# A dense SiLU feed-forward layer on one core: the first loads cut in two over both queues, the first group of matmuls taken by halves of the rows

## The chip, the cores and the metric

One NeuronCore of a Trainium2 chip runs the whole kernel in a single launch. The metric is the device time in microseconds, lower is better. The shorthand for the engines is that of the profile: PE is TensorE's matmul, PEld its weight load, DVE is VectorE, ACT is ScalarE, POOL is GpSimd, and SP is SyncE, which issues DMAs and computes nothing. A "q" behind an engine's name (SPq, ACTq) marks a DMA that this engine issued.

## The reference

All arrays are bf16. x has 2048 rows of 640, w1 is 640 x 1728, and w2 is 1728 x 640.

```python
def reference(x, w1, w2):
    h = jnp.einsum("bsd,df->bsf", x, w1)
    h = _silu(h)
    out = jnp.einsum("bsf,fd->bsd", h, w2)
    return out
```

## The kernel before, in words

**Shapes.** The contraction of the first product, 640, is five tiles of 128 (`dt` 0 to 4). The 1728 columns of w1 are thirteen full tiles of 128 (`ft` 0 to 12) and one half tile. The 2048 rows of x are four chunks of 512 (`sc` 0 to 3). The first product is made transposed: a matmul takes a 128x128 block of w1 as the stationary operand and 128x512 of the transposed x as the moving one, and five of them (one for each `dt`) add up in one of the eight PSUM banks. ACT takes the sigmoid out of the bank (L197) and DVE multiplies it with the bank (L200), which gives the hidden layer, transposed, in SBUF. The second product (L319) reads that as it lies.

**Order.** Nothing is scheduled by a program: `Plan.add` records the operations, each engine runs its own in the order in which they were added, and a wait is put before an operation whose dependence comes from another engine or from a DMA. Each engine's queue is in order, so what stands behind a waiting instruction waits too.

**The opening**, which is what the change touches. The first chunk of x (512 rows, four row tiles `j`) is loaded in plain form into `x0_sb` and transposed on PE with an identity (`transpose_x0`, L174), 128x128 at a time into a PSUM bank, from which one engine copies it to `xT_sb`: DVE for even `dt` (L178), ACT for odd ones (L180). `dt` 0 is done in two halves of two row tiles each, both copied by DVE; the other four are copied whole, 128x512. The other three chunks come transposed by DMA later (L235).

The DMAs of the opening are issued in this order. SP: x tile 0, row tiles 0 and 1 (64 KB); w1 tile 0 of the contraction, its first six column tiles (192 KB, `w1_0`); the same of w1 tiles 1 and 2; then, after a wait for both halves of x tile 0, w1 tiles 3 and 4; then the remaining columns of w1 in two pieces. ACT: x tile 0, row tiles 2 and 3 (64 KB); x tile 1 (128 KB); x tile 2 (128 KB); x tiles 3 and 4 together (256 KB); then the load of its sigmoid table and a small activation (L155).

PE's list at the opening is: six matmuls on constants whose results nobody reads (L164, five of 512 columns and one of 256); the four transposes of x tile 0; two more matmuls on constants (512 and 256 columns); and then the first column group, `column_group(0, ...)`: six column tiles of w1 in six banks, with the contraction tile as the outer loop, so that each of the thirty matmuls (L258) needs only the contraction tiles that have come so far. In each contraction tile, after the second of the six matmuls, the four transposes of the next x tile are put in (`between`). The first matmul of a contraction tile waits for the copied x tile and for its w1 tile. Behind the group come the column tiles 6 to 12 of the same rows (`unit`, L213), and then the other chunks.

The matmuls on constants use the last bank, the transposes of x tile 0 use banks 4 and 5, and those of the later x tiles use bank 6 or 7 in turn.

Of the kernel before, what the change touches and what calls it, by code (L numbers as in the profile page):

```python
# [20 lines left out]
class Plan:  # L21
# [53 lines left out]
def bass_standalone__dense_activation_silu__prompt_kernel(  # L75
# [6 lines left out]
    bf16 = mybir.dt.bfloat16  # L82
# [6 lines left out]
    P = 128  # L89
    H = P // 2  # L90
    SCH = 512
    DT = D // P
# [5 lines left out]
    JB = SCH // P  # L98
# [4 lines left out]
    with ExitStack() as es:  # L103
        def sb(name, shape, dtype):
            return es.enter_context(nc.sbuf_tensor(name, shape, dtype))

        xT_sb = sb("xT_sb", [P, DT, S], bf16)
        w1_sb = sb("w1_sb", [P, DT, F], bf16)
# [16 lines left out]
        add = plan.add  # L125
        bank_free = [[] for _ in range(NBANK)]
        turn = [0]

        def take_bank():
            b = turn[0] % NBANK  # L130
            turn[0] += 1
            return b


        FA = 6
        w1_cuts = [FA, 10, FT]
        id_a = add("pool", lambda e: e.memset(ident[:, :], 0.0))
        id_b = add("pool", lambda e: e.affine_select(
            out=ident[:, :], in_=ident[:, :], compare_op=ALU.not_equal, fill=1.0,
            base=0, pattern=[[-1, P]], channel_multiplier=1), [id_a])  # L140
        warm = add("dve", lambda e: e.memset(warm_sb[:, :], 0.0))

        def load_x0(eng, name, j0, j1, d0, d1):
            return add(eng, lambda e: e.dma_start(
                out=x0_sb[:, j0:j1, d0 * P:d1 * P], in_=x0_v[:, j0:j1, d0 * P:d1 * P]), group=name)

        def load_w1(eng, name, d0, d1, f0, f1, deps=()):
            return add(eng, lambda e: e.dma_start(
                out=w1_sb[:, d0:d1, f0:f1], in_=w1_v[:, d0:d1, f0:f1]), deps, group=name)

        x0_a = [load_x0("sp", "x0_a", 0, JB // 2, 0, 1), load_x0("act", "x0_b", JB // 2, JB, 0, 1)]
        w1_lo = [load_w1("sp", "w1_0", 0, 1, 0, FA * P)]
        x0_c = [load_x0("act", "x0_c", 0, JB, 1, 2), load_x0("act", "x0_d", 0, JB, 2, 3), load_x0("act", "x0_e", 0, JB, 3, DT)]
        w1_lo += [load_w1("sp", f"w1_{dt}", dt, dt + 1, 0, FA * P) for dt in (1, 2)]
        add("act", lambda e: e.activation(out=warm_sb[:, :], in_=warm_sb[:, :], func=ACT.Sigmoid), [warm])  # L155
        w1_lo += [load_w1("sp", f"w1_{dt}", dt, dt + 1, 0, FA * P, x0_a) for dt in (3, 4)]
        w1_dma = [load_w1("sp", f"w1_{name}", 0, DT, w1_cuts[g] * P, min(w1_cuts[g + 1] * P, F))
                  for g, name in enumerate("ab")]
# [3 lines left out]
        def warm_up(columns):  # L162
            for n in columns:
                add("pe", lambda e, n=n: e.matmul(  # L164
                    ps[:, NBANK - 1, 0:n], lhsT=ones[:, 0:P], rhs=ones[:, 0:n], start=True, stop=True))

        warm_up([SCH] * 5 + [2 * P])

        def transpose_x0(dt, j0, j1, b):

            dst = ps[:, b, :].bitcast(bf16)[:, j0 * P:j1 * P]
            out = xT_sb[:, dt, j0 * P:j1 * P]
            for j in range(j0, j1):
                t = add("pe", lambda e, j=j: e.transpose(  # L174
                    dst[:, (j - j0) * P:(j - j0 + 1) * P], x0_sb[:, j, dt * P:(dt + 1) * P], ident[:, :]),
                    [x0_a[j // (JB // 2)], id_b] if dt == 0 else [x0_c[min(dt, 3) - 1]] + bank_free[b])
            if dt % 2 == 0:
                c = add("dve", lambda e: e.tensor_copy(out=out, in_=dst), [t])  # L178
            else:
                c = add("act", lambda e: e.copy(out=out, in_=dst), [t])  # L180
            bank_free[b] = [c]
            return c

        def x_deps(sc, c0, n):
            return x0T if sc == 0 else x1_of if sc == 1 else [x_dma[sc]]

        def w1_deps(ft):
            return [w1_dma[max(g for g in range(len(w1_dma)) if w1_cuts[g] <= ft)]] if ft >= FA else w1_lo

        chunk_done, tail_done = {}, {}  # L190
        sig_free = [None] * NSIG
# [2 lines left out]
        def silu(b, parts, n, pe):  # L194
            s = sig_turn[0] % NSIG
            sig_turn[0] += 1
            a = add("act", lambda e: e.activation(  # L197
                out=sig_sb[:, s, 0:n], in_=ps[:, b, 0:n], func=ACT.Sigmoid), [pe, sig_free[s]])
            for rows, ft, cols in parts:
                v = add("dve", lambda e, rows=rows, ft=ft, cols=cols: e.tensor_tensor(  # L200
                    out=hT_sb[rows, ft, cols], in0=ps[rows, b, 0:n], in1=sig_sb[rows, s, 0:n],
                    op=ALU.mult), [a])
                chunk_done[cols.start // SCH] = v
                if ft == FR:
                    tail_done[cols.start // SCH] = v
            bank_free[b] = [v]
            sig_free[s] = v

        def unit(sc, ft, c0, n):
            b = take_bank()  # L210
            cols = slice(sc * SCH + c0, sc * SCH + c0 + n)
            for dt in range(DT):
                pe = add("pe", lambda e, dt=dt: e.matmul(  # L213
                    ps[:, b, 0:n], lhsT=w1_sb[:, dt, ft * P:(ft + 1) * P], rhs=xT_sb[:, dt, cols],
                    start=(dt == 0), stop=(dt == DT - 1)),
                    x_deps(sc, c0, n) + w1_deps(ft) + bank_free[b] if dt == 0 else ())
            silu(b, [(slice(0, P), ft, cols)], n, pe)

        def tail_unit(sc):
            b = take_bank()  # L220
            for dt in range(DT):
                for hh in range(2):
                    pe = add("pe", lambda e, dt=dt, hh=hh: e.matmul(  # L223
                        ps[hh * H:(hh + 1) * H, b, :], lhsT=w1_sb[:, dt, FR * P:F],
                        rhs=xT_sb[:, dt, (sc + hh) * SCH:(sc + hh + 1) * SCH],
                        start=(dt == 0), stop=(dt == DT - 1), skip_group_check=True),
                        x_deps(sc, 0, SCH) + x_deps(sc + 1, 0, SCH) + w1_deps(FR) + bank_free[b]
                        if dt == 0 else ())
            silu(b, [(slice(hh * H, (hh + 1) * H), FR, slice((sc + hh) * SCH, (sc + hh + 1) * SCH))
                     for hh in range(2)], SCH, pe)  # L230

        x_dma, x1_of, w2_dma = {}, [], []
        for sc in range(1, NSC):
            for dt in range(DT):
                x_dma[sc] = add("sp", lambda e, sc=sc, dt=dt: e.dma_start_transpose(  # L235
                    out=xT_sb[:, dt, sc * SCH:(sc + 1) * SCH],
                    in_=xf[sc * SCH:(sc + 1) * SCH, dt * P:(dt + 1) * P]),
# [3 lines left out]
            if sc == 2:  # L241
                half = FR // 2
                for a, z in ((0, half), (half, FR)):
                    w2_dma.append(add("sp", lambda e, a=a, z=z: e.dma_start(
                        out=w2_sb[:, a:z, :], in_=w2_v[:, a:z, :]), group="w2"))
                for hh in range(2):
                    w2_dma.append(add("sp", lambda e, hh=hh: e.dma_start(
                        out=w2_sb[hh * H:(hh + 1) * H, FR, :], in_=w2[FR * P:F, :]), group="w2"))

        def column_group(sc, x_dep, w1_dep, between=None):  # L250

            banks = [take_bank() for _ in range(FA)]
            for dt in range(DT):
                for ft in range(FA):
                    deps = bank_free[banks[ft]] if dt == 0 else []
                    if ft == 0:
                        deps = deps + [x_dep[dt], w1_dep[dt]]
                    pe = add("pe", lambda e, dt=dt, ft=ft: e.matmul(  # L258
                        ps[:, banks[ft], :], lhsT=w1_sb[:, dt, ft * P:(ft + 1) * P],
                        rhs=xT_sb[:, dt, sc * SCH:(sc + 1) * SCH],  # L260
                        start=(dt == 0), stop=(dt == DT - 1)), deps)
                    if dt == DT - 1:
                        silu(banks[ft], [(slice(0, P), ft, slice(sc * SCH, (sc + 1) * SCH))], SCH, pe)
                    if between and ft == 1:
                        between(dt + 1)

        def transpose_next(dt):
            if dt < DT:
                x0T.append(transpose_x0(dt, 0, JB, FA + dt % 2))

        half = [transpose_x0(0, k * JB // 2, (k + 1) * JB // 2, FA - 2 + k) for k in range(2)]
        x0T = [half[1]]
        warm_up([SCH, 2 * P])
        column_group(0, x0T, w1_lo, transpose_next)
        for ft in range(FA, FR):
            unit(0, ft, 0, SCH)

        for sc in range(1, NSC):
            if sc == 1:
                column_group(sc, x1_of, w1_lo)  # L280
            for ft in range(FA if sc == 1 else 0, FR):
                unit(sc, ft, 0, SCH)
        reg_done = dict(chunk_done)
# [111 lines left out]
```

## Time and profile before

| What | Value |
|---|---|
| three runs | 126.38, 126.88 and 129.13 us; median 126.88 |
| the profiled execution's own time | 126.5 us |
| its span, first to last instruction | 125.2 us |
| around the span | 1.3 us |
| PE busy | 122.1 us, 98% of the span |
| PEld busy | 57.4 us, 46% |
| DVE and ACT busy | 45.6 us (36%) and 39.4 us (32%) |
| DMA | 10.41 MB in 19625 packets |

The page has one part for each question: the busy time of each engine, the same in 40 slices, the DMA queues, the chain of work that ended last, the costliest groups of instructions, and the DMA issues with the median time from issue to landing. The trace also answers by stretches of time (the timeline, in which neighbouring instructions of one line are merged: start, length, engine, line, names, count, and in brackets the idle time before and what ended it). A landing below is the start of the issue plus the time to landing. The end of a matmul is modelled and reaches into the next one, so what the array takes for one matmul is read from the distance between two starts.

### The profile page before, as it was taken

The page shows a single profiled execution, that of the slowest core. Times are in us where ns is not written, and L with a number is a line of the kernel's source. Part 1 is how long each engine was busy: PE and PEld are TensorE (multiplying, and loading weights), DVE is VectorE, ACT ScalarE, POOL GpSimd, SP SyncE. Part 2 cuts the span into 40 slices and gives each one's busy share as a digit, 9 for nine tenths or more (in the row PEclk, how much of TensorE's full clock was granted, in tenths as well). Part 3 has the DMA queues.
Part 4 walks back from the last instruction along what each step waited for, and adds up shares of the span by engine and source line. Part 5 has one row for each costly group of instructions (what it writes and reads, how often), then busy time and mean ns, then how long its engine had stood idle before and what let it go on. Part 6 is the DMA issues. An engine that isn't in the chain of part 4 may idle for free.

```text
span 125.2 us, 2101 instructions
## 1 busy us (share of the span) xinstructions
PE 122.1 (98%) x902; PEld 57.4 (46%) x902; DVE 45.6 (36%) x72; ACT 39.4 (32%) x69; POOL 0.7 (1%) x6
## 2 busy tenths in 40 slices
PE   7999999999999999999999999999999999999992
PEld 2544444444444444444444444444444444445481
DVE  0112986069766666666673020202020120202022
ACT  0523953087555555555540010101010110101021
POOL 2000000000000000000000000000000000000000
PEclk9999999999999999999999999999999999999999
DMA  3995355589910000000000001114120200112424
GB/s 77 314 385 181 86 113 72 112 237 390 276 43 0 5 0 0 3 0 0 0 0 5 0 0 31 26 22 168 52 105 5 105 0 21 26 21 73 157 98 117
DMA packets 19625, 10.41 MB, mean 83 GB/s; under 512 B 13344, under 2 KB 19616, under 8 KB 19616
## 3 DMA queue, kind: packets, MB, share of 16 engines
q1 hardware_dynamic: 17472, 9.56, 26.6%
q10 hardware_dynamic: 2144, 0.72, 2.2%
q8 instruction: 7, 0.11, 0.4%
q14 instruction: 2, 0.02, 0.1%
HBM read 5.16 MB, written 2.62 MB: 62 GB/s over the span
## 4 chain that ended last, share of the span: by engine, by line
PE 98%; DVE 0%; issue 0%
PE ps L319 47%; PE ps L213 34%; PE ps L258 11%; PE ps L164 3%; PE ps L223 2%; PE ps L174 1%; DVE o_sb L330 0%
## 5 line engine op out<-in xcount | busy, mean ns | idle before, releaser
L319 PE MATMUL ps<-w_sb,hT_sb 64*128 64x512 bf16 (+2 forms) x486 | 47.3, 352 | 0.0
L200 DVE TENSOR_TENSOR hT_sb<-ps,sig_sb 128x512 bf16<-128x512 f32 (+1 forms) x56 | 37.0, 688 | 19.0 <-ACT sig_sb L197 18.9
L213 PE MATMUL ps<-xT_sb,w_sb 128*128 128x512 bf16 x200 | 43.5, 379 | 0.0
L197 ACT ACTIVATE sig_sb<-ps 128x512 bf16<-128x512 f32 x54 | 30.7, 606 | 24.9 <-PE ps L213 16.4
L319 PEld LDWEIGHTS ps<-w_sb,hT_sb 64*128 64x128 bf16 x486 | 23.3, 94 | 23.7
L213 PEld LDWEIGHTS ps<-xT_sb,w_sb 128*128 128x128 bf16 x200 | 19.6, 98 | 23.6
L330 DVE CAST o_sb<-ps 128x512 bf16<-128x512 f32 (+2 forms) x9 | 5.7, 632 | 37.6 <-PE ps L319 37.6
L332 ACT CAST o_sb<-ps 128x512 bf16<-128x512 f32 (+2 forms) x9 | 4.8, 538 | 38.6 <-PE ps L319 38.6
L258 PE MATMUL ps<-xT_sb,w_sb 128*128 128x512 bf16 x60 | 14.4, 387 | 0.0
L319 PE MATMUL ps<-hT_sb,w_sb 64*128 64x512 bf16 x108 | 12.3, 376 | 0.0
L258 PEld LDWEIGHTS ps<-xT_sb,w_sb 128*128 128x128 bf16 x60 | 5.6, 99 | 6.7 <-DVE xT_sb L178 0.7
L319 PEld LDWEIGHTS ps<-hT_sb,w_sb 64*128 64x128 bf16 x108 | 5.2, 94 | 6.6 <-issue 0.4
L330 DVE CAST oT_sb<-ps 128x512 bf16<-128x512 f32 x2 | 1.4, 692 | 11.7 <-PE ps L319 11.7
L332 ACT CAST oT_sb<-ps 128x512 bf16<-128x512 f32 x2 | 1.2, 586 | 13.6 <-PE ps L319 13.6
L178 DVE COPY xT_sb<-ps 128x256 bf16<-128x256 bf16 (+1 forms) x4 | 1.4, 358 | 8.6 <-PE ps L174 8.6
L164 PE MATMUL ps<-const-bfloat16-1.0 128*128 128x512 bf16 (+1 forms) x8 | 3.3, 572 | 0.8 <-PEq L380 0.8
L174 PEld LDWEIGHTS ps<-ident,x_sb 128*128 128x128 bf16 x20 | 1.9, 115 | 1.7 <-DMA x_sb<-in_x_dram 0.7
L174 PE MATMUL ps<-ident,x_sb 128*128 128x128 bf16 x20 | 2.4, 256 | 0.0
L180 ACT COPY xT_sb<-ps 128x512 bf16<-128x512 bf16 x2 | 1.2, 585 | 3.9 <-PE ps L174 3.9
L223 PE MATMUL ps<-xT_sb,w_sb 128*64 128x512 bf16 x20 | 2.3, 381 | 0.0
L155 ACT ACT_TABLE_LOAD x1 | 1.3, 1283 | 2.9 <-issue 2.9
L164 PEld LDWEIGHTS ps<-const-bfloat16-1.0 128*128 128x128 bf16 x8 | 1.0, 137 | 1.9 <-issue 1.9
(9 smaller groups left out, 2.3 us busy)
## 6 DMA issues: line engine op xcount, KB each, us to landing
out_dram<-o_sb SPq DMA_DIRECT2D x14, 160.0 KB, 1.9
w_sb<-in_w_dram SPq DMA_DIRECT2D x1, 1120.0 KB, 7.6
w_sb<-in_w_dram SPq DMA_DIRECT2D x5, 192.0 KB, 4.8
w_sb<-in_w_dram SPq DMA_DIRECT2D x1, 960.0 KB, 5.3
w_sb<-in_w_dram SPq DMA_DIRECT2D x1, 640.0 KB, 6.3
w_sb<-in_w_dram SPq DMA_DIRECT2D x1, 560.0 KB, 7.3
x_sb<-in_x_dram ACTq DMA_DIRECT2D x2, 128.0 KB, 3.8
x_sb<-in_x_dram ACTq DMA_DIRECT2D x1, 256.0 KB, 5.8
```

Source lines behind the costliest of these rows:

```text
L155: add("act", lambda e: e.activation(out=warm_sb[:, :], in_=warm_sb[:, :], func=ACT.Sigmoid), [warm])
L164: add("pe", lambda e, n=n: e.matmul(ps[:, NBANK - 1, 0:n], lhsT=ones[:, 0:P], rhs=ones[:, 0:n], start=True, stop=True))
L174: t = add("pe", lambda e, j=j: e.transpose(dst[:, (j - j0) * P:(j - j0 + 1) * P], x0_sb[:, j, dt * P:(dt + 1) * P], ident[:, :]), [x0_a[j ...
L178: c = add("dve", lambda e: e.tensor_copy(out=out, in_=dst), [t])
L197: a = add("act", lambda e: e.activation(out=sig_sb[:, s, 0:n], in_=ps[:, b, 0:n], func=ACT.Sigmoid), [pe, sig_free[s]])
L200: v = add("dve", lambda e, rows=rows, ft=ft, cols=cols: e.tensor_tensor(out=hT_sb[rows, ft, cols], in0=ps[rows, b, 0:n], in1=sig_sb[rows, ...
L213: pe = add("pe", lambda e, dt=dt: e.matmul(ps[:, b, 0:n], lhsT=w1_sb[:, dt, ft * P:(ft + 1) * P], rhs=xT_sb[:, dt, cols], start=(dt == 0), ...
L223: pe = add("pe", lambda e, dt=dt, hh=hh: e.matmul(ps[hh * H:(hh + 1) * H, b, :], lhsT=w1_sb[:, dt, FR * P:F], rhs=xT_sb[:, dt, (sc + hh) * ...
L258: pe = add("pe", lambda e, dt=dt, ft=ft: e.matmul(ps[:, banks[ft], :], lhsT=w1_sb[:, dt, ft * P:(ft + 1) * P], rhs=xT_sb[:, dt, sc * SCH:( ...
L319: pe = add("pe", lambda e, b=b, n=n, lhsT=lhsT, rhs=rhs, ft=ft: e.matmul(ps[:, b, 0:n], lhsT=lhsT, rhs=rhs, start=(swap == 0 and ft == 0), ...
L330: ev = add("dve", lambda e, b=b, n=n, dst=dst: e.tensor_copy(out=dst, in_=ps[:, b, 0:n]), [pe])
L332: ev = add("act", lambda e, b=b, n=n, dst=dst: e.copy(out=dst, in_=ps[:, b, 0:n]), [pe])
```

## The change

Three things are done in the opening; from the second column group on the code does what it did.

1. The loads. `w1_0`, 192 KB, becomes two DMAs of 96 KB: column tiles 0 to 2 on SP, 3 to 5 on ACT. x tile 1, 128 KB, becomes two of 64 KB: row tiles 0 and 1 on SP, 2 and 3 on ACT. SP so has x tile 0 (first half), w1_0 (first half), x tile 1 (first half), w1 tiles 1 and 2, and the rest as before. ACT has x tile 0, w1_0 and x tile 1 (second halves each), x tile 2, x tiles 3 and 4, and then its table.
2. The first contraction tile of the first column group is done by halves of the rows: six matmuls of 256 columns for the first 256 rows and six for the other 256, in place of six of 512. Each waits only for its half of x and its half of w1_0. The transposes of x tile 1 now stand behind the fourth of the twelve. The second of the two matmuls on constants ahead of the group, the one of 256 columns, is left out.
3. Each x tile is transposed into two banks (4 and 5 for tile 0, 6 and 7 for all others), two row tiles in each, and copied as two pieces of 128x256: both by DVE for tile 0, one by DVE and one by ACT for the others.

```diff
-        w1_lo = [load_w1("sp", "w1_0", 0, 1, 0, FA * P)]
-        x0_c = [load_x0("act", "x0_c", 0, JB, 1, 2), load_x0("act", "x0_d", 0, JB, 2, 3), load_x0("act", "x0_e", 0, JB, 3, DT)]
-        w1_lo += [load_w1("sp", f"w1_{dt}", dt, dt + 1, 0, FA * P) for dt in (1, 2)]
+        w1_0 = [load_w1("sp", "w1_0a", 0, 1, 0, FA // 2 * P), load_w1("act", "w1_0b", 0, 1, FA // 2 * P, FA * P)]
+        x0_b = [load_x0("sp", "x0_c", 0, JB // 2, 1, 2), load_x0("act", "x0_d", JB // 2, JB, 1, 2)]
+        x0_c = [load_x0("act", "x0_e", 0, JB, 2, 3), load_x0("act", "x0_f", 0, JB, 3, DT)]
+        w1_lo = [load_w1("sp", f"w1_{dt}", dt, dt + 1, 0, FA * P) for dt in (1, 2)]
...
-        def transpose_x0(dt, j0, j1, b):
-
-            dst = ps[:, b, :].bitcast(bf16)[:, j0 * P:j1 * P]
-            out = xT_sb[:, dt, j0 * P:j1 * P]
-            for j in range(j0, j1):
-                t = add("pe", lambda e, j=j: e.transpose(
-                    dst[:, (j - j0) * P:(j - j0 + 1) * P], x0_sb[:, j, dt * P:(dt + 1) * P], ident[:, :]),
-                    [x0_a[j // (JB // 2)], id_b] if dt == 0 else [x0_c[min(dt, 3) - 1]] + bank_free[b])
-            if dt % 2 == 0:
-                c = add("dve", lambda e: e.tensor_copy(out=out, in_=dst), [t])
-            else:
-                c = add("act", lambda e: e.copy(out=out, in_=dst), [t])
-            bank_free[b] = [c]
-            return c
+        def transpose_x0(dt, b0):
+
+            copies = []
+            for h in range(2):
+                dst = ps[:, b0 + h, :].bitcast(bf16)[:, 0:SCH // 2]
+                out = xT_sb[:, dt, h * (SCH // 2):(h + 1) * (SCH // 2)]
+                load = (x0_a[h], x0_b[h], x0_c[0], x0_c[1], x0_c[1])[dt]
+                for k in range(2):
+                    t = add("pe", lambda e, k=k, h=h, dst=dst: e.transpose(
+                        dst[:, k * P:(k + 1) * P], x0_sb[:, 2 * h + k, dt * P:(dt + 1) * P], ident[:, :]),
+                        [load, id_b] + bank_free[b0 + h])
+                if h == 0 or dt == 0:
+                    c = add("dve", lambda e, dst=dst, out=out: e.tensor_copy(out=out, in_=dst), [t])
+                else:
+                    c = add("act", lambda e, dst=dst, out=out: e.copy(out=out, in_=dst), [t])
+                bank_free[b0 + h] = [c]
+                copies.append(c)
+            return copies
...
             for dt in range(DT):
-                for ft in range(FA):
-                    deps = bank_free[banks[ft]] if dt == 0 else []
-                    if ft == 0:
-                        deps = deps + [x_dep[dt], w1_dep[dt]]
...
+                by_half = between is not None and dt == 0
+                for h in range(2 if by_half else 1):
+                    c0, c1 = (h * (SCH // 2), (h + 1) * (SCH // 2)) if by_half else (0, SCH)
+                    for ft in range(FA):
+                        deps = [x_dep[dt][h], w1_dep[dt][ft >= FA // 2]] if by_half else []
+                        if not by_half and ft == 0:
+                            deps = x_dep[dt] + w1_dep[dt]
+                        if dt == 0 and h == 0:
+                            deps = deps + bank_free[banks[ft]]
+                        pe = add("pe", lambda e, dt=dt, ft=ft, h=h, c0=c0, c1=c1: e.matmul(
+                            ps[:, banks[ft], c0:c1], lhsT=w1_sb[:, dt, ft * P:(ft + 1) * P],
+                            rhs=xT_sb[:, dt, sc * SCH + c0:sc * SCH + c1],
+                            start=(dt == 0 and h == 0), stop=(dt == DT - 1), skip_group_check=True), deps)
+                        if dt == DT - 1:
+                            silu(banks[ft], [(slice(0, P), ft, slice(sc * SCH, (sc + 1) * SCH))], SCH, pe)
+                        if between and h == 0 and ft == (3 if by_half else 1):
+                            between(dt + 1)
...
-        half = [transpose_x0(0, k * JB // 2, (k + 1) * JB // 2, FA - 2 + k) for k in range(2)]
-        x0T = [half[1]]
-        warm_up([SCH, 2 * P])
-        column_group(0, x0T, w1_lo, transpose_next)
+        x0T = [transpose_x0(0, FA - 2)]
+        warm_up([SCH])
+        w1_of = [w1_0] + [[d] for d in w1_lo]
+        column_group(0, x0T, w1_of, transpose_next)
```

More of the change, by code (lines that the diff above doesn't have):

```diff
@@ L167, in bass_standalone__dense_activation_silu__prompt_kernel @@
         warm_up([SCH] * 5 + [2 * P])
-        def transpose_x0(dt, j0, j1, b):
-            dst = ps[:, b, :].bitcast(bf16)[:, j0 * P:j1 * P]
-            out = xT_sb[:, dt, j0 * P:j1 * P]
-            for j in range(j0, j1):
-                t = add("pe", lambda e, j=j: e.transpose(
-                    dst[:, (j - j0) * P:(j - j0 + 1) * P], x0_sb[:, j, dt * P:(dt + 1) * P], ident[:, :]),
-                    [x0_a[j // (JB // 2)], id_b] if dt == 0 else [x0_c[min(dt, 3) - 1]] + bank_free[b])
-            if dt % 2 == 0:
-                c = add("dve", lambda e: e.tensor_copy(out=out, in_=dst), [t])
-            else:
-                c = add("act", lambda e: e.copy(out=out, in_=dst), [t])
-            bank_free[b] = [c]
-            return c
+        def transpose_x0(dt, b0):
[15 more added lines that the diff above has]
+            return copies
         def x_deps(sc, c0, n):
-            return x0T if sc == 0 else x1_of if sc == 1 else [x_dma[sc]]
+            return x0T[-1] if sc == 0 else x1_of if sc == 1 else [x_dma[sc]]
         def w1_deps(ft):
-            return [w1_dma[max(g for g in range(len(w1_dma)) if w1_cuts[g] <= ft)]] if ft >= FA else w1_lo
+            return [w1_dma[max(g for g in range(len(w1_dma)) if w1_cuts[g] <= ft)]] if ft >= FA else w1_lo[-1:]
         chunk_done, tail_done = {}, {}
@@ L253, in column_group @@
             for dt in range(DT):
-                for ft in range(FA):
-                    deps = bank_free[banks[ft]] if dt == 0 else []
-                    if ft == 0:
-                        deps = deps + [x_dep[dt], w1_dep[dt]]
[L258 to L265, printed above, removed]
+                by_half = between is not None and dt == 0
@@ L267, in transpose_next @@
         def transpose_next(dt):
             if dt < DT:
-                x0T.append(transpose_x0(dt, 0, JB, FA + dt % 2))
-        half = [transpose_x0(0, k * JB // 2, (k + 1) * JB // 2, FA - 2 + k) for k in range(2)]
-        x0T = [half[1]]
-        warm_up([SCH, 2 * P])
-        column_group(0, x0T, w1_lo, transpose_next)
+                x0T.append(transpose_x0(dt, FA))
+        x0T = [transpose_x0(0, FA - 2)]
+        warm_up([SCH])
+        w1_of = [w1_0] + [[d] for d in w1_lo]
+        column_group(0, x0T, w1_of, transpose_next)
@@ L279, in bass_standalone__dense_activation_silu__prompt_kernel @@
             if sc == 1:
-                column_group(sc, x1_of, w1_lo)
+                column_group(sc, [[d] for d in x1_of], w1_of)
             for ft in range(FA if sc == 1 else 0, FR):
```

## The prediction

> **What bounds the kernel now.** I read the page's busy times and its chain first, then the timeline of the first 13 us, then the DMA issues one by one.
>
> ```profile
> span 125.2 us, 2101 instructions
> PE 122.1 (98%) x902; PEld 57.4 (46%) x902; DVE 45.6 (36%) x72; ACT 39.4 (32%) x69; POOL 0.7 (1%) x6
> ...
> PE 98%; DVE 0%; issue 0%
> PE ps L319 47%; PE ps L213 34%; PE ps L258 11%; PE ps L164 3%; PE ps L223 2%; PE ps L174 1%; DVE o_sb L330 0%
> ```
>
> PE is the whole chain. The change can gain only where PE does something useless (L164, constants) or waits, and that is the opening:
>
> ```profile
> 0.77 2.50 PE L164 MATMUL ps<-const-bfloat16-1.0 128*128 128x512 bf16 x6 [0.77 <-PEq L380]
> ...
> 3.07 0.63 PE L174 MATMUL ps<-ident,x_sb 128*128 128x128 bf16 x4
> ...
> 3.50 0.84 PE L164 MATMUL ps<-const-bfloat16-1.0 128*128 128x512 bf16 x2
> 3.53 0.51 DVE L178 COPY xT_sb<-ps 128x256 bf16<-128x256 bf16 x2 [2.63 <-PE ps L174]
> ...
> 4.34 0.14 PEld L258 LDWEIGHTS ps<-xT_sb,w_sb 128*128 128x128 bf16 x2 [0.69 <-DVE xT_sb L178]
> 4.37 1.01 PE L258 MATMUL ps<-xT_sb,w_sb 128*128 128x512 bf16 x2
> ...
> 5.17 0.63 PE L174 MATMUL ps<-ident,x_sb 128*128 128x128 bf16 x4
> ...
> 5.60 1.51 PE L258 MATMUL ps<-xT_sb,w_sb 128*128 128x512 bf16 x6
> ...
> 8.46 0.39 PE L174 MATMUL ps<-ident,x_sb 128*128 128x128 bf16 x4
> ...
> 8.68 1.46 PE L258 MATMUL ps<-xT_sb,w_sb 128*128 128x512 bf16 x6
> ```
>
> Two things are to be seen. First, the array runs at two paces. Four transposes and the matmul behind them start 0.43 us after the first transpose at 5.17 (to 5.60), but 0.22 at 8.46 (to 8.68); 512 columns take 427 ns up to about 5.7 us, and 216 behind it (six in 1.46 us, five distances and a last end of 379). The profile's granted clock reads 1.00 in both stretches, so here the pace comes from the durations. Second, from 4.37 us on PE has no gap that counts. The first real matmul stands at 4.37; its x was copied by 4.04 (3.53 + 0.51), so DVE, which the line names, was not what it waited for. It was the load of w1_0:
>
> ```profile
> w_sb<-in_w_dram SPq DMA_DIRECT2D x1, 192.0 KB, 3.0
> ...
> x_sb<-in_x_dram ACTq DMA_DIRECT2D x1, 256.0 KB, 5.8
> ```
>
> These are two narrow cuts of the DMA view. w1_0, issued at 1.25, lands at 4.23; the matmul follows 0.14 later. x tiles 3 and 4, issued at 2.35, land at 8.17, and the transposes of x tile 3 start at 8.46: the one later load with little slack.
>
> **The change part by part.** The sum is made against the profiled execution, 126.5 us, which is 0.38 below the median of the three runs, 126.88, and 0.12 above the lowest.
>
> *The 256 constant columns left out.* The constants of 512 columns start at 3.50 and leave the array free at 3.93 (427 ns), where the 256 begin today and last until 4.14. The first real matmul can start at 3.93 at the earliest, 0.44 us before today, if its data are there. Until 5.7 us the array is at half pace, so 0.44 us of earlier start is only 0.22 us of work at the later pace: the most that this change can bring.
>
> *w1_0 in two halves on two queues.* The trace of before has no such load. Below: x tile 0's halves of 64 KB landed 2.2 us after issue, which puts a half of w1_0 issued at 1.25 at 3.45. Above: x tile 1 (128 KB on ACT, issued at 1.26 beside w1_0) took 3.3 us: 4.6. Nearest is w1_0 itself, as the two halves together are its bytes: 4.23. I take 4.05, a little of the way towards the small load, because two queues start at once. Then the first matmul starts at 4.05 + 0.14 = 4.19, and the gain is (4.37 - 4.19) / 2 = 0.09 us. With the two ends it is 0.22, or a loss of (4.74 - 4.37) / 2 = 0.18. Against this speaks a rule of the Trainium skill, "DMA: Bandwidth & Descriptors", Rules for kernel authors: spreading DMAs over the issuing queues brings no bandwidth, since all run on the same 16 engines and interleave. The trace agrees in part: the stretch from 3.07 to 4.37 us shows a DMA share of 1.03. By that rule alone both halves land at 4.23, the gain is nothing, and the sum below becomes 126.5 with no minus.
>
> *Twelve matmuls of 256 for six of 512.* The columns are the same. Four transposes of 128 take 223 ns at the later pace where one matmul of 512 takes 216, so an instruction more costs 2.5 ns: six cost 0.015 us, and none at half pace (4 x 107 = 427). Weight loads are covered even at 56 ns from start to start. The fourth matmul waits for the ACT half of w1_0, and the transposes of x tile 1 stand behind it: 4 x 213 = 0.85 us after the start, at 5.04. The halves of x tile 1 come behind the halves of w1_0; today the whole landed at 4.6. If they land by 4.9 nothing waits; that leaves 0.3 us.
>
> *Copies by two engines.* A 128x256 copy takes 0.29 us on DVE, 128x512 takes 0.43 on DVE and 0.59 on ACT. Today the matmul that needs an ACT copy still starts on the beat: the copy of tile 3 ends at 9.47 and the matmul starts at 9.55, 216 ns after its neighbour. A shorter copy takes away a stall that is not there: 0. ACT's copy of tile 1 has before it one DMA issue more (0.5 us), the table load and the small activation: they end at 4.43 today, 4.95 then, and the copy is needed at about 5.7. Covered.
>
> *Issues moved.* SP has one DMA more before w1 tiles 1 and 2: half a microsecond later in issue, against landings at 5.14 (needed at 6.51) and 6.99 (needed at 8.03). Tiles 3 and 4 wait today for x tile 0 after a pause of 0.4 us, which takes up the extra issue. On ACT, x tile 2 landed at 6.14 and is needed at 6.94: 0.8 us of slack for an issue 0.55 later. x tiles 3 and 4 are issued 0.55 us later too, behind 32 KB more on their queue. Bounds: 8.17 as today, 8.17 + 0.55 = 8.72 if the issue sets it. The queue is far behind the issue (5.8 us), so the bytes should set it: 32 KB at the 286 GB/s of that stretch is 0.11, giving 8.28. A load has to land 0.14 before its user, so today's limit is 8.46 - 0.14 = 8.32, and it moves forward with the gain. The end therefore shifts by the greater of -0.09 and 8.28 - 8.32 = -0.04. With the extra instructions that is -0.03: 126.5 - 0.03 = 126.47, rounded 126.5. The next thing to be late is this load, and it eats half of the gain.
>
> **The rivals.**
>
> *All as drawn, and x tiles 3 and 4 in time.* The start is at 3.93: -0.22 + 0.015 gives 126.3. For it: 64 KB loads land in 2.2 us. Against it: the DMA share of 1.03 at that time.
>
> *The halves land together, no earlier than w1_0 today.* The array idles where the constants were, and the gain is zero: 126.5. That the split does not do what it says is this case.
>
> *Slower: x tiles 3 and 4 set the pace.* Place: the wait of the transposes of x tile 3. It decides from a landing behind 8.32; at 8.72 the price is 0.40: 126.9. For it: the margin of 0.15. Against it: 5.8 us between issue and landing.
>
> *Slower: the fast pace comes late.* Today PE idles for 0.23 us (4.14 to 4.37) before the pace doubles at 5.7, 4.9 us after the first matmul. Without the 256 columns the idle stretch is (start - 3.93), 0.26 by my landing and up to 0.8 by the upper end. It decides if that is too much idleness for whatever doubles the pace; 0.23 is all that this trace shows to be harmless. If a stretch as long as the first is then run at half pace, half of 4.9 us is lost: 126.5 + 2.45 = 129.0. The Trainium skill ("TensorE: Matmul & The Clock Gate", Part 1) has a free-running window of 3.4 us that must be busy; by an estimate from that figure the loss is 1.7 us, and 128.2. No view here shows where a window begins, and by that page the same kernel shifts from run to run.
>
> **How the numbers follow.** The forecast with the early case: 0.50, from 126.3 to 126.5, the value 126.5. No gain: 0.20, 126.5. Tiles 3 and 4 late: 0.20, up to 126.9. Late pace: 0.10, up to 129.0. The first three are of one sign or none and lie within 0.6 us, so the range comes rather from how executions differ: the lowest run is 0.5 below the median, and the median 0.38 above the profiled one. Low: 126.3 - 0.4 = 125.9. High: 126.9 + 0.8 (twice the 0.38) = 127.7. Left out are the late pace (0.10) and a tenth for runs such as the 129.13. Two per cent of 126.88 is 2.5 us, about what a measurement of this kernel can tell from no change. Faster by that: no case reaches it, 0.01 for the runs' spread. Slower: the late pace at its full price and over, 0.04. Within: 0.95.
>
> **What would show it.** The start of the first real matmul between 3.93 and 4.37, the landing of the first half of w1_0 near 4.05, the 256-column matmuls 213 ns apart, the doubling of the pace near 5.7, the transposes of x tile 3 at 8.4 without a gap on PE before them, and the first matmul of the column tiles behind the group a few hundredths ahead of today's 12.36. What would make it wrong: PE gaps above 0.3 us at the x tiles 1 to 3, or a pace that doubles a microsecond or more from 5.7.

## The result, and the profile after

Over 17 runs each, the changed kernel takes 127.21 us in the median (126.54 to 128.30) and the kernel before 126.30 (125.67 to 129.13). The ratio of the times is 1.0073, with a 95% interval of 1.0050 to 1.0096: the change costs about 0.9 us. (The ratios here and below leave out runs that took over 1.5 per cent more than the fastest of their kernel.) The forecast was 126.5 us, a shift of -0.03. The profiled execution of the changed kernel took 127.55 us over a span of 126.2; that of the kernel before had 126.5 and 125.2.

The page of the changed kernel, with the same lines as those of before:

```profile
span 126.2 us, 2117 instructions
PE 121.8 (96%) x907; PEld 57.5 (46%) x907; DVE 45.9 (36%) x74; ACT 39.8 (32%) x71; POOL 0.7 (1%) x6
...
PE 91%; DMA 5%; ACTq 2%; DVE 0%; issue 0%
PE ps L331 46%; PE ps L218 34%; PE ps L270 8%; DMA x_sb<-in_x_dram 5%; PE ps L228 2%; ACTq L144 1%; PE ps L178 0%; ACTq L148 0%; DVE o_sb L342 0%
```

PE's own work is 0.3 us less, and it is no longer the whole chain: a load of x and ACT's issues have come into it. The chain of the first 21 us, in order of time (start, length, what), says which:

```profile
1.27 0.49 ACTq L148
1.76 0.03 issue
1.79 0.46 ACTq L144
2.25 0.03 issue
2.28 0.49 ACTq L144
2.77 0.03 issue
2.80 6.66 DMA x_sb<-in_x_dram
9.46 0.04 issue
9.50 0.40 PE ps L178 x4
```

This is to be read from below. The transposes of x tile 3 start at 9.50, when x tiles 3 and 4 have landed (9.46); that load was issued at 2.80 as ACT's fifth, and the chain goes on through the issues ahead of it, because ACT could not issue it sooner. Before, the same transposes started at 8.46. Behind them nothing differs: from them to the first matmul of the column tiles behind the group it is 3.91 us in the changed kernel (9.50 to 13.41) and 3.90 before (8.46 to 12.36). So the 1.04 us at this place are the whole of the longer span. PE's timeline shows the other waits:

```profile
3.93 0.64 PE L270 MATMUL ps<-xT_sb,w_sb 128*128 128x256 bf16 x4
4.40 0.61 PE L178 MATMUL ps<-ident,x_sb 128*128 128x128 bf16 x4
4.85 1.04 PE L270 MATMUL ps<-xT_sb,w_sb 128*128 128x256 bf16 x8
6.55 0.59 PE L270 MATMUL ps<-xT_sb,w_sb 128*128 128x512 bf16 x2 [0.67 <-DMA w_sb<-in_w_dram]
7.35 0.40 PE L178 MATMUL ps<-ident,x_sb 128*128 128x128 bf16 x4 [0.21 <-DMA x_sb<-in_x_dram]
...
9.50 0.40 PE L178 MATMUL ps<-ident,x_sb 128*128 128x128 bf16 x4 [0.46 <-DMA x_sb<-in_x_dram]
```

The opening does start sooner: the first real matmul stands at 3.93, not 4.37. In this execution the pace also doubled early, at 4.0 us (the 256-column matmuls start 0.11 apart, not 0.21), where the profile of before has 5.7. All that was won there is then waited for, three times, each time for a load: w1 tile 1, x tile 2, x tiles 3 and 4. (A fourth wait, 0.2 us, lies within the row at 4.40: the second half of x tile 1 landed at 4.68.)

### The profile page after: what moved, and what is told of

It reads as the page before. It is cut to its first block, busy times and chain, and to the rows that moved or that the text cites. A ratio compares the mean times of both kernels' runs of the same rounds, so it can differ in the third digit from the quotient of the medians.

```text
span 126.2 us, 2117 instructions
## 1 busy us (share of the span) xinstructions
PE 121.8 (96%) x907; PEld 57.5 (46%) x907; DVE 45.9 (36%) x74; ACT 39.8 (32%) x71; POOL 0.7 (1%) x6
## 4 chain that ended last, share of the span: by engine, by line
PE 91%; DMA 5%; ACTq 2%; DVE 0%; issue 0%
PE ps L331 46%; PE ps L218 34%; PE ps L270 8%; DMA x_sb<-in_x_dram 5%; PE ps L228 2%; ACTq L144 1%; PE ps L178 0%; ACTq L148 0%; DVE o_sb L342 0%
## 5 line engine op out<-in xcount | busy, mean ns | idle before, releaser
L218 PE MATMUL ps<-xT_sb,w_sb 128*128 128x512 bf16 x200 | 43.5, 379 | 0.0
L218 PEld LDWEIGHTS ps<-xT_sb,w_sb 128*128 128x128 bf16 x200 | 19.6, 98 | 23.6
L270 PE MATMUL ps<-xT_sb,w_sb 128*128 128x512 bf16 (+1 forms) x66 | 14.1, 360 | 0.7 <-DMA w_sb<-in_w_dram 0.7
L270 PEld LDWEIGHTS ps<-xT_sb,w_sb 128*128 128x128 bf16 x66 | 6.2, 99 | 6.8 <-issue 0.9
L182 DVE COPY xT_sb<-ps 128x256 bf16<-128x256 bf16 x6 | 1.7, 292 | 9.1 <-PE ps L178 9.1
L184 ACT COPY xT_sb<-ps 128x256 bf16<-128x256 bf16 x4 | 1.5, 372 | 5.5 <-PE ps L178 5.5
```

What stands on the lines that cost most here:

```text
L182: c = add("dve", lambda e, dst=dst, out=out: e.tensor_copy(out=out, in_=dst), [t])
L184: c = add("act", lambda e, dst=dst, out=out: e.copy(out=out, in_=dst), [t])
L218: pe = add("pe", lambda e, dt=dt: e.matmul(ps[:, b, 0:n], lhsT=w1_sb[:, dt, ft * P:(ft + 1) * P], rhs=xT_sb[:, dt, cols], start=(dt == 0), ...
L270: pe = add("pe", lambda e, dt=dt, ft=ft, h=h, c0=c0, c1=c1: e.matmul(ps[:, banks[ft], c0:c1], lhsT=w1_sb[:, dt, ft * P:(ft + 1) * P], rhs= ...
```

## The experiments

**Two theories.** Theory L: the loss lies in the loads; Theory P: it lies on PE's side (constants left out, halves, two banks). Then, within the loads: the order on SP (Q), the number of loads (N), slow first reads of w1 (F), and the number of issues that stand ahead of a load on its queue (I). The table has all kernels; "issues" counts those added ahead of the later opening loads on SP and on ACT, "tile 3" is when the load that the transposes of x tile 3 wait for has landed, and "GB/s" is what the DMAs moved from 3.6 to 5.2 us. These two columns come from one profile each, and they vary: before, pe_only and act_last issue the same loads up to that one in the same order, and it landed at 8.17, 7.14 and 7.49. The ratios come from 6 to 14 runs (17 for the changed kernel) beside runs of the kernel before.

| Kernel | Issues SP, ACT | Tile 3, us | GB/s | Ratio to before, 95% interval |
|---|---|---|---|---|
| before | 0, 0 | 8.17 | 299 | 1 |
| changed | 1, 1 | 9.46 | 174 | 1.0073, 1.0050 to 1.0096 |
| loads_only | 1, 1 | 9.70 | 235 | 1.0061, 1.0036 to 1.0085 |
| pe_only | 0, 0 | 7.14 | 304 | 0.9999, 0.9976 to 1.0023 |
| w1_split | 0, 1 | 8.97 | 307 | 1.0037, 1.0019 to 1.0055 |
| x1_split | 1, 0 | 8.82 | 196 | 1.0059, 1.0033 to 1.0086 |
| x1_on_act | 0, 1 | 9.12 | 242 | 1.0044, 1.0018 to 1.0070 |
| x1_behind | 1, 0 | 7.52 | 269 | 1.0128, 1.0071 to 1.0185 |
| touch | 1, 2 | 8.75 | 272 | 1.0114, 1.0066 to 1.0163 |
| x3_x4 | 1, 1 | 8.00 | 150 | 1.0045, 1.0025 to 1.0066 |
| act_late | 0, 1 | 8.75 | 312 | 1.0066, 1.0029 to 1.0102 |
| sp_late | 1, 0 | 8.75 | 233 | 1.0075, 1.0044 to 1.0106 |
| x34_pool | 0, 1 | 7.01 | 281 | 1.0150, 1.0098 to 1.0201 |
| touch_pool | 1, 1 | 9.54 | 112 | 1.0159, 1.0123 to 1.0196 |
| act_last | 0, 0 | 7.49 | 288 | 0.9999, 0.9972 to 1.0025 |
| act_late2 | 0, 2 | 8.88 | 307 | 1.0128, 1.0088 to 1.0169 |
| swap | -1, 0 | 7.00 | 331 | 1.0126, 1.0084 to 1.0167 |
| swap_before | -1, 0 | 6.90 | 326 | 1.0072, 1.0036 to 1.0109 |
| swap_warm | -1, 0 | 6.75 | 327 | 1.0018, 0.9997 to 1.0038 |
| x4_sp | 0, 0 | 6.80 | 314 | 0.9984, 0.9963 to 1.0004 |

### One side of the change alone: loads_only and pe_only

loads_only is the kernel before with the four split loads (the diff's first hunk) and waits for both halves of each. pe_only is the changed kernel with the loads of before:

```diff
-        w1_0 = [load_w1("sp", "w1_0a", 0, 1, 0, FA // 2 * P), load_w1("act", "w1_0b", 0, 1, FA // 2 * P, FA * P)]
-        x0_b = [load_x0("sp", "x0_c", 0, JB // 2, 1, 2), load_x0("act", "x0_d", JB // 2, JB, 1, 2)]
+        w1_0 = [load_w1("sp", "w1_0", 0, 1, 0, FA * P)] * 2
+        x0_b = [load_x0("act", "x0_c", 0, JB, 1, 2)] * 2
```

> The kernel before with the four split loads alone; PE's list, the transposes and the copies are those of before, the first matmul waits for both halves of w1 tile 0. Theory L (the split loads make x tiles 3 and 4 land about 1.2 us later than the 8.17 of before, and PE waits at the transposes of x tile 3): the whole loss comes back, about +0.9 us, ratio near 1.007, landing of x tiles 3 and 4 behind 9.0 us and a PE wait of 0.5 to 1 us ahead of them. Theory P (the loss lies on PE's side: the constants left out, the halves, two banks): ratio 1.000 within 0.2%, landing near 8.2 us.

> The changed kernel with the loads of before: w1 tile 0 in one piece on SP, x tile 1 in one piece on ACT; halves of the rows, two banks, copies by two engines and the constants left out stay. Theory L: no loss, 126.1 to 126.4 us beside a before of 126.3, ratio 0.998 to 1.001, x tiles 3 and 4 land near 8.2 us. Theory P: the loss stays, ratio near 1.007, although the loads land as in before.

loads_only has the loss (1.0061; x tiles 3 and 4 at 9.70), pe_only has none (0.9999; 7.14 where 8.2 was expected). Theory P falls: halves, two banks, copies by two engines and the missing constants together are worth nothing that 12 runs can show, in either direction.

### One load split at a time: w1_split and x1_split

Each is the changed kernel with one of the two lines above put back.

> The changed kernel, but x tile 1 is one load on ACT; w1 tile 0 stays in halves on both queues. Theory L with the ACT queue as the cause (bytes and issues ahead of x tiles 3 and 4 on ACT's queue): ACT has 96 KB and one issue more than before, the most of all, so the loss is at least that of the change, ratio 1.007 to 1.010, landing of x tiles 3 and 4 at 9.5 us or later. If the split of x tile 1 is the cause instead: ratio 1.000 to 1.002, landing near 8.2 us.

> The changed kernel, but w1 tile 0 is one load on SP; x tile 1 stays in halves on both queues. Theory L with the ACT queue as the cause: ACT has 64 KB less than before ahead of x tiles 3 and 4 and no issue more, so they land at 8.2 us or earlier and the ratio is 0.997 to 1.001; w1 tile 1, now behind 64 KB more on SP, may make PE wait up to 0.3 us. If the split of x tile 1 is the cause instead: ratio near 1.007.

Both lose, 1.0037 and 1.0059. w1_split lies between its two expected cases and fits neither; x1_split fits its second case. The ACT queue alone is not the cause: x1_split has less on ACT than the kernel before, and x tiles 3 and 4 are late all the same (8.82). What the two have in common is one issue more, w1_split on ACT and x1_split on SP.

### Order, number, first reads: x1_on_act, x1_behind, touch, x3_x4

```diff
 # x1_on_act: against x1_split
-        x0_b = [load_x0("sp", "x0_c", 0, JB // 2, 1, 2), load_x0("act", "x0_d", JB // 2, JB, 1, 2)]
+        x0_b = [load_x0("act", "x0_c", 0, JB // 2, 1, 2), load_x0("act", "x0_d", JB // 2, JB, 1, 2)]
 # touch: against the changed kernel, ahead of all loads
...
+        add("act", lambda e: e.dma_start(out=touch_sb[:, :, :], in_=w1_v[:, :, 0:16]), group="touch")
 # x3_x4: against the changed kernel
-        x0_c = [load_x0("act", "x0_e", 0, JB, 2, 3), load_x0("act", "x0_f", 0, JB, 3, DT)]
+        x0_c = [load_x0("act", "x0_e", 0, JB, 2, 3), load_x0("act", "x0_f", 0, JB, 3, 4), load_x0("act", "x0_g", 0, JB, 4, DT)]
...
```

x1_behind is x1_split with the two SP lines for x tile 1 and w1 tile 1 exchanged.

> The changed kernel with w1 tile 0 in one load on SP, and both halves of x tile 1 on ACT: as many DMAs as in the kernel x1_split, but SP's queue holds w1 tile behind w1 tile as before the change. Theory Q (the x load between two w1 loads on SP is what slows the stream): ratio 0.998 to 1.002, the stretch from 3.6 to 5.2 us at about 300 GB/s, x tiles 3 and 4 land by 8.3 us. Theory N (more and smaller loads slow it, wherever they stand): ratio 1.004 to 1.007, the stretch at 200 to 240 GB/s.

> The kernel x1_split with one place changed: on SP the half of x tile 1 stands behind w1 tile 1, not ahead of it. Theory Q: w1 tiles 0 and 1 run through, ratio 1.000 to 1.002, the stretch from 3.6 to 5.2 us near 300 GB/s; the half of x tile 1 lands near 5.2 us in place of 4.4, which may make PE wait 0.2 us. Theory N: ratio 1.005 to 1.007 as in x1_split (same loads, same number).

> The changed kernel with one load more, ahead of all others on ACT: 16 columns of each row of all five w1 tiles (20 KB in 640 pieces of 32 bytes) into a buffer that nobody reads. Theory F (the first read of a part of w1 is slow, and in the changed kernel this is paid when PE waits): the slow packets of w1 tile 1 and later, 0.4 to 1.5 us in the changed kernel, are gone, the stretch from 4.1 to 5.7 us (half a microsecond later for the extra issue) is near 300 GB/s, ratio 1.000 to 1.004. If slow packets come from something else: they stay, the stretch is at 170 to 240 GB/s, and half a microsecond of issue comes on top: ratio 1.007 to 1.012.

> The changed kernel with x tiles 3 and 4 in two loads of 128 KB in place of one of 256 KB, tile 3 first. If the end is set by the landing that the transposes of x tile 3 wait for, as in the profile of the changed kernel (9.46 us, a wait of 0.6 us), tile 3 lands 0.5 us or more earlier and the ratio falls from 1.007 to 1.001 to 1.004, with what is left waiting for w1 tile 1 and x tile 2. If more loads cost (theory N): ratio 1.007 to 1.010.

Theory Q falls with x1_on_act: SP's queue is that of before, and the kernel still loses (1.0044). x1_behind came out against both theories, 1.0128. Its late loads were early (x tiles 3 and 4 at 7.52), but the SP half of x tile 1 landed at 6.30, and PE stood still for it:

```profile
4.27 0.60 PE L271 MATMUL ps<-xT_sb,w_sb 128*128 128x256 bf16 x4 [0.21 <-DMA w_sb<-in_w_dram]
6.34 0.40 PE L179 MATMUL ps<-ident,x_sb 128*128 128x128 bf16 x4 [1.47 <-DMA x_sb<-in_x_dram]
```

That is a load with three others ahead of it on its queue, late again.

x3_x4 does what its first theory said, in part: tile 3 lands at 8.00 in place of 9.46, with PE now waiting for the second half of x tile 1 (until 5.3) and for x tile 2 (until 7.2). The loss is 0.45 per cent in place of 0.7, where at most 0.4 was expected; the two intervals overlap, so the fall itself is not clear of noise.

touch is a case of its own. The DMA rate came back (272 GB/s from 3.6 to 5.2 us, although ACT's loads are issued 0.5 us later than in the changed kernel), and in the trace's packet records the slow reads of w1 became fewer (packets up to 13 us that took more than twice the median of their size: 45 in the changed kernel, 23 here, 21 before). This speaks for Theory F in the stream. The time did not follow, because x tile 0 landed late and the pace doubled late:

```profile
3.07 0.42 PE L180 MATMUL ps<-ident,x_sb 128*128 128x128 bf16 x2
4.25 0.39 PE L180 MATMUL ps<-ident,x_sb 128*128 128x128 bf16 x2 [0.76 <-DMA x_sb<-in_x_dram]
...
6.14 2.77 PE L272 MATMUL ps<-xT_sb,w_sb 128*128 128x256 bf16 x10
8.70 0.45 PE L180 MATMUL ps<-ident,x_sb 128*128 128x128 bf16 x4
```

Eight matmuls of 256 columns and two of 512 take 2.56 us from 6.14 to 8.70, which is 213 and 427 ns each: half pace, until 8.8 us.

### One issue more and no bytes: act_late, sp_late, act_last, act_late2

Here 512 bytes that nobody reads are loaded at one place in the kernel before; nothing else differs.

```diff
 # act_late (act_late2: twice; act_last: behind all x tiles; sp_late: on SP between w1 tiles 0 and 1)
...
-        x0_c = [load_x0("act", "x0_c", 0, JB, 1, 2), load_x0("act", "x0_d", 0, JB, 2, 3), load_x0("act", "x0_e", 0, JB, 3, DT)]
+        x0_c = [load_x0("act", "x0_c", 0, JB, 1, 2)]
+        add("act", lambda e: e.dma_start(out=late_sb[:, :], in_=xf[0:16, 0:16]), group="late")
+        x0_c += [load_x0("act", "x0_d", 0, JB, 2, 3), load_x0("act", "x0_e", 0, JB, 3, DT)]
```

> The kernel before with one tiny load more (512 bytes, nobody reads it) on ACT between x tile 1 and x tile 2: no byte moves, but x tiles 2 to 4 are issued half a microsecond later, as in the changed kernel. Theory I (what is issued later lands later by as much or more, the number of issues ahead is what counts): x tiles 3 and 4 land at 8.7 to 9.2 us in place of 8.17, ratio 1.003 to 1.005. If the bytes on the queue set the landing, as the prediction had it: landing at 8.2 us, ratio 1.000.

> The kernel before with the same tiny load on SP between w1 tiles 0 and 1: w1 tiles 1 and 2 are issued half a microsecond later. Theory I: w1 tile 1 lands near 5.7 and tile 2 near 7.5 us, which PE needs at 6.5 and 8.0: ratio 1.000 to 1.001, x tiles 3 and 4 at 8.2 us. If a pause in SP's stream of w1 brings slow packets back (theory S): w1 tile 1 lands at 6.4 us or later, the stretch from 3.6 to 5.2 us falls from 300 to 200 or 240 GB/s, ratio 1.004 to 1.006.

> The kernel before with the tiny load of act_late (512 bytes, nobody reads it) on ACT behind all x tiles, so that no load is issued later; only the table load moves by 0.5 us, which has cover. Theory I (later issue, later landing): ratio 1.000 within 0.2%, x tiles 3 and 4 land near 8.2 us. If one more load disturbs the stream wherever it stands (theory N): ratio 1.004 to 1.007 as in act_late.

> The kernel before with two such tiny loads on ACT between x tile 1 and x tile 2: x tiles 2 to 4 are issued about 1 us later. Theory I: x tiles 3 and 4 land at 9.2 us or later, about another 0.5 us behind act_late, ratio 1.009 to 1.014. Theory N without a dose: ratio near that of act_late, 1.005 to 1.008.

With one tiny load on ACT the ratio is 1.0066, with one on SP 1.0075, as much as with the whole change. Behind all other loads of ACT it costs nothing (0.9999). With two it is 1.0128. It is thus not the bytes, and not that there is one load more, but how many stand ahead of the loads that PE needs. The chain of act_late shows one such delay (L155 is the tiny load):

```profile
1.79 0.52 ACTq L155
2.32 0.03 issue
2.35 0.45 ACTq L144
2.79 0.03 issue
2.82 5.93 DMA x_sb<-in_x_dram
8.75 0.05 issue
8.80 0.40 PE ps L177 x4
```

The tiny load takes ACT 0.52 us to issue, as long as one of 128 KB. x tiles 3 and 4 are issued 0.47 us later than before (2.82 for 2.35) and land 0.58 later (8.75 for 8.17). PE waits 0.2 us for x tile 2 and 0.3 us for x tiles 3 and 4. This profile is 0.3 us longer than that of before, while the medians differ by 0.75 us; what the rest of the loss is made of, this one profile does not show. With two tiny loads x tile 2 lands at 7.93 (6.95 with one, 6.14 before), and PE waits 1.5 us for it; x tiles 3 and 4 land at 8.88, only 0.13 behind act_late, where 9.2 or later was expected.

In sp_late the step is larger: w1 tile 1 is issued 0.47 later, at 2.22, and lands 1.81 later, at 6.95, and PE waits for it from 6.6 to 7.1:

```profile
5.42 1.36 PE L260 MATMUL ps<-xT_sb,w_sb 128*128 128x512 bf16 x4
7.08 0.59 PE L260 MATMUL ps<-xT_sb,w_sb 128*128 128x512 bf16 x2 [0.30 <-DMA w_sb<-in_w_dram]
```

(The idle time in brackets counts from the modelled end of the matmul before.) Theory I had expected a landing near 5.7 and no loss here; the landing and the 233 GB/s are the signs of the other theory in that expectation, by which a pause in SP's stream of w1 brings slow reads back. These reads became hardly more (28, with 29 in act_late and 21 before), so that its cause is not shown either. And x tiles 3 and 4, which ACT issues at 2.35 as before, landed at 8.75 as in act_late (8.82 in x1_split, which has its issue more on SP too). An issue more on one queue thus goes with later landings on the other as well; by what way is not shown.

### POOL's queue: x34_pool and touch_pool

```diff
 # x34_pool: against w1_split
-        x0_c = [load_x0("act", "x0_e", 0, JB, 2, 3), load_x0("act", "x0_f", 0, JB, 3, DT)]
+        x0_c = [load_x0("act", "x0_e", 0, JB, 2, 3), load_x0("pool", "x0_f", 0, JB, 3, DT)]
 # touch_pool: against the changed kernel, behind the identity
...
+        touch = add("pool", lambda e: e.dma_start(out=touch_sb[:, :, :], in_=w1_v[:, :, 0:16]), group="touch")
+        add("pool", lambda e: e.memset(touch_sb[:, :, :], 0.0), [touch])
```

> The kernel w1_split with x tiles 3 and 4 issued by POOL in place of ACT, behind the identity: ACT then issues its half of w1 tile 0, x tile 1 and x tile 2, and is done 0.5 us earlier. If the late landing of x tiles 3 and 4 behind the added issue is what the split of w1 costs: they land at 8.3 us or earlier and the ratio falls from 1.004 to 0.998 to 1.001. If the slow packets of w1 set it: ratio 1.003 to 1.006, landing at 9 us.

> The changed kernel with the early read of 16 columns of each w1 row (20 KB, into a buffer that nobody uses) issued by POOL behind the identity, so that no issue of SP or ACT moves. Theory F (first reads of w1 are slow, and an early touch takes that off the loads PE waits for): w1 tile 1 lands by 5.7 us in place of 6.4, x tiles 3 and 4 by 8.8 in place of 9.5, the stretch from 3.6 to 5.2 us is at 240 to 300 GB/s in place of 174, ratio 1.001 to 1.004. If only the later issue counts (theory I): landings as in the changed kernel, ratio 1.006 to 1.009.

Both expectations were missed, 1.0150 and 1.0159. In x34_pool tiles 3 and 4 landed early (7.01), but x tile 1 landed at 5.68 and x tile 2 at 7.65 (4.60 and 6.14 before), and PE waited for w1 tile 0 and for these two. In touch_pool the touch itself landed only at 6.39, and the DMAs moved 112 GB/s meanwhile. The profile of x34_pool is that of its fastest run (127.23 us; the median is 128.18), so it shows only part of the loss. With a load on POOL, w1 tile 1 and x tile 2 came later in both than in the kernel that each was made from; why is not shown. For Theory F touch_pool is no support: the slow reads of w1 fell to 23 as in touch, and w1 tile 1 landed no earlier (6.94 for 6.42).

### One issue less, and the pace: swap, swap_before, swap_warm, x4_sp

```diff
 # swap (against the changed kernel, x tile 1 whole on ACT) and, in the same way, swap_before (against the kernel before)
...
+        x0_a = [load_x0("sp", "x0_a", 0, JB, 0, 1)] * 2
+        w1_0 = [load_w1("act", "w1_0", 0, 1, 0, FA * P)] * 2
 # swap_warm: against swap_before
-        warm_up([SCH] * 5 + [2 * P])
+        warm_up([SCH] * 7 + [2 * P])
 # x4_sp: against the kernel before; tile 4 behind w1 tile 2
...
+        x0_c.append(load_x0("sp", "x0_f", 0, JB, 4, DT))
...
```

> The changed kernel's PE side with other loads: x tile 0 whole (128 KB) first on SP, w1 tile 0 whole first on ACT, then x tiles 1, 2, 3 and 4 on ACT and w1 tiles 1 to 4 on SP. One load less than in the kernel before, w1 tiles 0 to 2 issued 0.5 us earlier, the x tiles as before. Theory I: w1 tile 0 lands near 3.8 us, w1 tile 1 near 4.7, x tiles 3 and 4 at 8.2 or earlier; ratio 0.996 to 0.999. If the order does not matter: 1.000. Against it: x tile 0 in 128 KB lands later than its halves, near 3.3 us in place of 3.1, and PE waits 0.2 us at its first transposes.

> The kernel before with the same loads as in swap. Theory I: ratio 0.997 to 1.000 (its first matmul stands behind the 256 constant columns, so less of an early landing is used). The difference between swap and swap_before is what the PE side of the change is worth when its loads are in time: at most the 0.2 us of the prediction, so 0.002.

> The kernel swap_before with two more matmuls of 512 columns on constants ahead of the transposes of x tile 0, which fill PE's wait for that load (0.85 us, to about 3.93). If the idle stretch delays the doubling of the pace (the rival of the late pace): it doubles near 5.7 us again, in place of 7.1, and the ratio falls from 1.007 to 1.000 to 1.003 (the first real matmul still stands 0.6 us later than in the kernel before, half of which is lost). If the idle stretch is not the cause: the ratio stays at 1.006 to 1.010.

> The kernel before with x tiles 3 and 4 in two loads: tile 3 where both were on ACT, tile 4 on SP behind w1 tile 2, in the pause in which SP waits for x tile 0. No load that is needed soon is issued later. Theory I: x tile 3 lands near 7.5 us in place of 8.17, the other landings stay; a gain only where the pace doubles early and PE waited for it, ratio 0.997 to 1.000. Theory N (one more load disturbs): 1.004 or more.

With one issue less on SP, w1 tile 1 landed at 4.80 and 4.84 (5.14 before) and x tiles 3 and 4 at 7.00 and 6.90, as Theory I says, the DMAs at 331 and 326 GB/s; x tile 1 did not come earlier (4.99 and 5.00 for 4.60), nor x tile 2 (6.24 and 6.14 for 6.14). Yet both kernels were slower, 1.0126 and 1.0072, where a gain or nothing was expected. x tile 0 in one piece landed at 3.92, and PE, done with its constants, stood still. PE's timeline of swap:

```profile
0.77 2.51 PE L165 MATMUL ps<-const-bfloat16-1.0 128*128 128x512 bf16 x6 [0.77 <-PEq L392]
3.96 0.61 PE L178 MATMUL ps<-ident,x_sb 128*128 128x128 bf16 x4 [0.69 <-DMA x_sb<-in_x_dram]
...
6.08 2.76 PE L270 MATMUL ps<-xT_sb,w_sb 128*128 128x256 bf16 x10
8.63 0.63 PE L178 MATMUL ps<-ident,x_sb 128*128 128x128 bf16 x4
```

The transposes at 8.63 are still at half pace (four and the next start in 0.43 us). swap_warm fills that wait with two more matmuls on constants:

```profile
0.77 3.35 PE L164 MATMUL ps<-const-bfloat16-1.0 128*128 128x512 bf16 x8 [0.77 <-PEq L380]
...
4.50 0.84 PE L164 MATMUL ps<-const-bfloat16-1.0 128*128 128x512 bf16 x2
5.14 0.93 PE L258 MATMUL ps<-xT_sb,w_sb 128*128 128x512 bf16 x2
5.91 0.39 PE L174 MATMUL ps<-ident,x_sb 128*128 128x128 bf16 x4
```

At 5.91 the pace is the full one (0.39 for four transposes), and the ratio falls from 1.0072 to 1.0018, although the first real matmul comes later (5.14 for 5.02). By the ratios, useless work at that place is worth about 0.5 per cent, 0.7 us; the two intervals just touch. In the profiles of all these kernels the pace doubled anywhere from 4.0 to 9.5 us. The Trainium skill, "TensorE: Matmul & The Clock Gate", Part 1, has the clock doubled after a busy window of about 3.4 us that runs free of the kernel. The spread of these times is compatible with that (the earliest, 4.0 us, is 3.2 us behind PE's first matmul), but no run here shows where a window begins.

x4_sp uses the pause of 0.5 us in which SP waits for x tile 0 (2.64 to 3.17 in the kernel before): it issues x tile 4 there, so that ACT's last load is tile 3 alone and nothing else is issued more than 0.2 us later. Tile 3 lands at 6.80; the median is 126.13 us beside 126.27 for the kernel before, 0.9984 with an interval of 0.9963 to 1.0004. It is faster than the changed kernel, and not clear of the kernel before. So one load more, of itself, costs nothing. Its profile is of its slowest run (126.98 us): PE has no early hole and waits for no load behind the first matmul, but the pace doubles only at 6.8 us. The time of the doubling thus also moves the time of one and the same kernel.

## Why the prediction was wrong, point by point

**The constants left out: right as far as the start goes.** The first real matmul came at 3.93, the earliest that was named. Whether the 0.22 us were won cannot be told: the pace doubled early in this profile, PE waited behind it, and pe_only, where the constants are left out too, has an interval of 0.3 us to either side.

**The halves of w1_0: no gain shown.** 4.05 was taken; 3.73 and 3.88 were measured, in w1_split 4.39 and 4.58. Over all profiles, the whole landed at 3.76 to 4.56 in the ten kernels in which SP issues it second, and both halves by 3.81 to 4.58 in the six in which the two queues issue them second. The Trainium skill ("DMA: Bandwidth & Descriptors", Rules for kernel authors) says that spreading loads over the queues brings no bandwidth; these landings agree.

**Twelve matmuls of 256 and the copies: right.** The eight from 4.85 start 0.11 us apart; a 128x256 copy took 0.29 us on DVE and 0.37 on ACT. (The prediction's 2.5 ns for an instruction more is 2.3 by its own rows, 7 ns over three instructions; the sum does not change.) pe_only puts the whole PE side at 0.9999.

**The issues moved: wrong, and this is the step that failed.** It read: "The queue is far behind the issue (5.8 us), so the bytes should set it: 32 KB at the 286 GB/s of that stretch is 0.11, giving 8.28." Measured: 9.46, outside both ends that were given (8.17 and 8.72). act_late, sp_late and act_last show what stands in its place: an issue more that moves hardly any bytes costs the kernel 0.7 per cent when it stands ahead of the loads that PE needs, on either queue, and nothing when it stands behind them. The landings go the same way: 7.14 to 8.17 in the three kernels with no issue more, and 8.75 to 9.70 in ten of the eleven that have one or more added and load x tiles 3 and 4 as one on ACT; the eleventh is x1_behind (7.52), where PE waits for another load. The long time from issue to landing was taken for a reserve, and no run shows one: behind a later issue it was 5.93 us in act_late, where before it was 5.82 and in pe_only and act_last 4.79 and 5.13. With L = 9.46 the prediction's own formula, the greater of the gain and the landing against 8.32, gives +1.1; the span grew by 1.0. The formula was right and one term of it was mis-sized by 1.2 us. The signs that the prediction named for being wrong came: a wait of PE above 0.3 us at x tile 3 (0.46, and 0.67 for w1 tile 1), and a pace that doubled over a microsecond from 5.7. That the measured median lies inside the stated range is luck: its upper end is the late case, 126.9, with 0.8 us for the scatter of runs on top, and the loss was over twice that case's price of 0.4.

**w1 tile 1 and x tile 2: wrong for the same reason.** They were passed over because issues half a microsecond later stood against slacks of 1.4 and 0.8 us. They landed 1.28 and 1.16 us later (6.42 for 5.14, 7.30 for 6.14), and PE waited for both, the more so as it came early.

**The rivals.** The one that came is "x tiles 3 and 4 set the pace", with 0.20 and a price of 0.40; it cost 0.9. The late pace did not come in the profile of the changed kernel (4.0 us). It is real, though: touch, swap and swap_before have it, with 7.1 to 9.5 us.

**What stays open.** Only part of the delay is the issue itself (0.45 to 0.49 us of 1.16 to 1.29). In the changed kernel the DMAs moved 174 GB/s from 3.6 to 5.2 us where the kernel before has 299:

```profile
3.60:5.20 1.60, 1.57 (x6) 0.36 (x5) 0.43 (x2) 0.82 (x2) 0.00 (x0) 1.00 1.09 299
```

```profile
3.60:5.20 1.60, 1.55 (x15) 1.03 (x13) 0.73 (x3) 1.42 (x3) 0.00 (x0) 1.00 0.94 174
```

(The first is of before, the second of the changed kernel; the last two columns are DMA share and GB/s.) The engines were nearly as busy and moved less: single reads of w1 took up to 1.5 us. act_late kept 312 GB/s and lost as much, sp_late had 233, so the lower rate is no condition of the loss. In touch and touch_pool the slow reads of w1 were half as many, and neither kernel was faster. Landings come from one profile of each kernel, and how an issue on one queue delays a load of the other is open. Whether the tiny load delays by the time of its issue alone or also by what it occupies on its queue was not told apart.

## What to carry to other kernels

In an opening that is fed by two queues, count the issues ahead of each load that an engine will wait for, not the bytes: a split load is one issue more for everything behind it, here 0.5 us each, on either queue. Where nothing that is needed soon stands behind it, a load more costs nothing (act_last, x4_sp). A time from issue to landing is no slack; slack is the landing against the start of the user, and it was 0.3 us here for the last load. And before taking filler work off PE, look whether it covers a wait: a hole in the first microseconds can cost more than the filler (swap_before beside swap_warm), though not every hole does (0.56 us in pe_only, and no loss).

## What the runs showed of the hardware that was not expected

A load of 512 bytes takes as long to issue as one of 128 KB (0.52 us on ACT), and one of them ahead of the others cost the kernel 0.66 per cent (0.29 to 1.02), two 1.28 (0.88 to 1.69). PE's pace doubled at 7.1 to 9.5 us in the three profiles in which PE stood idle for 0.69 to 0.76 us ahead of 4.3 us (touch, swap, swap_before), and between 4.0 and 6.8 us in the others, among them pe_only with 0.56 us of idleness up to 4.69, while the granted clock in the profile's rows read 1.00 from 3.6 to 5.2 us at either pace.
